# Three edits to the first stage of a fused sparse-attention and MoE kernel: which queue carries the weight words, where one copy stands, and which rounds convert weights

## The chip, the cores and the metric

The kernel runs on one core of a Trainium2 chip. Five engines with instruction streams of their own work side by side: TensorE (PE, matrix products; its weight loads are listed as PEld), VectorE (DVE), ScalarE (ACT), GpSimd (POOL) and SyncE (SP). Each executes its stream strictly in order. Loads and stores are carried by 16 DMA engines; SP, ACT and POOL issue them, and what each of the three issues stands in a queue of its own (q1 for SP, q10 for ACT, q0 for POOL). The metric is the device time of one execution in microseconds (us); lower is better.

## The reference, cut to what matters

```
scores = q @ k.T / sqrt(64)            # 4 batches, 8 heads, 768 positions, 64 wide
mask: own and neighbouring blocks of 32, first and last block, 3 sampled blocks per block;
      the first and the last block see everything
attn = softmax(scores where mask) ;  x = attn @ v          # x: 3072 tokens x 512
h = x @ w_in                                               # 512 -> 2048
g = h * sigmoid(1.702 * h)
out = g @ w_out                                            # 2048 -> 512
```

All products are made to full float32 accuracy by splitting operands into a high and a low part of a reduced format, so that one product is three matmuls.

## The kernel before, in words

Attention is cut into units of 64 query rows. A unit of the first and last block is dense and is worked in two items; every other unit is sparse and is one item. An item has scores (L342 dense, L332 sparse, on PE), a row maximum (`least`: L355 or L349 and its negation `nm`, on DVE), exponentials (`exps`, L366 or L363, on ACT), transposes through PE (L381) whose results ACT copies out of PSUM as tiles `pt` (L387), values (L419 dense, L410 sparse, on PE), a normalisation (L426 to L436, DVE), and a turn of the finished x (L443 on PE, then the high part on ACT, L450, and the low part on DVE, L451).

The first stage (`first`) works 13 items: three in `opening`, then one loop round for each of items 3 to 12; below, a round has its item's number. Item 3 is the second half of a dense unit, items 4 and 5 are sparse, 6 to 9 dense, 10 to 12 sparse. A round n makes the scores and the maximum of item n, transposes and copies item n-1, turns a finished unit, makes item n's exponentials and the values of item n-2 (in the last three rounds also of item n-1).

Between these stand the weights' operations. The generator `weights` turns w_in and w_out (64-bit words, so loaded as tiles `raw` of twice the size) into pairs of high and low parts. Each tile takes four steps: a shift on DVE (L524), a merge on DVE (L526) after which ACT's first pass (L486) of the next tile is put down, the low part of the tile before (L494), and a second merge on DVE (L535) after which ACT's cast (L501) is put down. ACT's share and the loads of later tiles wait in a list, `late`, that `flush` empties, at the latest at a round's end. w_out's merged tile is also stored to a scratch tensor `ws` (L503). Five tiles' conversions and a little are done in the first stage; the rest is spread over the first 16 steps of the second stage, which runs the MoE products (L574 to L576 up, L621 to L626 down) densely on PE with the remaining sparse items in between.

The words are loaded by ACT's queue in both stages (L476). All other loads of the first stage, those of the keys (`kres`, `kg`), the queries (`qt`), the dense values (`vown<-in_vd_dram`) and the middle rows (`vmid`), stand in SP's queue; the gathered rows of v come by POOL's. A load waits until its buffer is free and until the load eight before it, of SP's and ACT's together, has landed.

Of the kernel before, what the change touches and what calls it, by code (L numbers as in the profile page):

```python
# [54 lines left out]
class Kernel:  # L55
# [93 lines left out]
    def indices(self):  # L149
# [8 lines left out]
        def take(shape):  # L158
            n = 1
            for k in shape:  # L160
# [9 lines left out]
        nc.vector.tensor_copy(out=d[0:1], in_=self.sbr)  # L170
        vblk = take([NB])
        first, second = slice(1, NB - 2, 2), slice(2, NB - 1, 2)
        nc.gpsimd.iota(vblk[3 * BLK:P, first], pattern=[[2, NU]], base=-NB, channel_multiplier=0,
                       allow_small_or_imprecise_dtypes=True)
# [31 lines left out]
        for i in range(NR):  # L206
            for cols, rows in ((first, slice(BLK * i, BLK * (i + 1))), (second, slice(BLK * (i + 1), BLK * (i + 2)))):
                nc.vector.tensor_copy(out=vblk[rows, cols], in_=rr[rows, cols, i])
# [248 lines left out]
    def weights(self):  # L457

        nc = self.nc
        todo = []  # L460
        for f in range(NF + LAG):
            if f < NF:
                todo.append((f, 0))
            if f >= LAG:
                todo.append((f - LAG, 1))
        self.ready = set()
        tiles = {}

        scalar = self.late.append
        asked = [0]  # L470

        def fetch(k):
            def go(k, own):
                f, i = todo[k]
                raw = self.raw4 if own else self.words.tile([P, 2 * DM], I32, name="raw", bufs=3)
                nc.scalar.dma_start(out=raw, in_=self.w64[i][f])  # L476
                tiles[k] = {"raw": raw.rearrange("p (a b) -> p a b", b=2)}

            for n in range(asked[0], min(k + 1 + self.early, len(todo))):
                scalar(lambda n=n, own=self.early and n % 4 == 3: go(n, own))  # L480
                asked[0] += 1

        def first(k):
            def go():
                a = tiles[k]["a"] = self.words.tile([P, DM], I32, name="a", bufs=3)
                nc.scalar.activation(out=a.bitcast(F32), in_=tiles[k]["raw"][:, :, 1].bitcast(F32), func=AF.Abs, scale=REBASE)  # L486

            if k < len(todo):
                scalar(go)

        def last(k):
            f, i = todo[k]
            t, w = tiles[k]["t"], tiles[k]["a"].bitcast(F32)
            nc.vector.tensor_tensor(out=t[:, DM:2 * DM], in0=w, in1=t[:, 0:DM].bitcast(F32), op=ALU.subtract)  # L494
            self.ready.add((f, i))

        def high(k):
            def go():
                f, i = todo[k]
                t, w = tiles[k]["t"], tiles[k]["a"].bitcast(F32)  # L500
                nc.scalar.copy(out=t[:, 0:DM], in_=w)  # L501
                if i == 1:
                    nc.scalar.dma_start(out=self.ws[f], in_=w)  # L503
                tiles[k]["high"] = True

            scalar(go)

        fetch(0)
        yield
        fetch(1)  # L510
        first(0)
        yield
        for k, (f, i) in enumerate(todo):
            while i == 1 and f - WRING > self.downs - 1:
                yield
            fetch(k + 2)
            if i == 0 and f == NWIN:
                self.opening.close()
                late = self.pool("late", 1)
                self.win += [late.tile([P, 2 * DM], F32R, name=f"win{n}") for n in range(NWIN, NF)]  # L520
            if "a" not in tiles[k]:
                self.flush()
            raw, a = tiles[k]["raw"], tiles[k]["a"]
            nc.vector.tensor_scalar(out=a, in0=a, scalar1=3, scalar2=None, op0=ALU.logical_shift_left)  # L524
            yield
            nc.vector.scalar_tensor_tensor(out=a, in0=raw[:, :, 1], scalar=-0x80000000, in1=a, op0=ALU.bitwise_and,  # L526
                                           op1=ALU.bitwise_or)
            first(k + 1)
            yield
            if k > 0:  # L530
                if "high" not in tiles[k - 1]:
                    self.flush()
                last(k - 1)
            yield
            nc.vector.scalar_tensor_tensor(out=a, in0=raw[:, :, 0], scalar=29, in1=a, op0=ALU.logical_shift_right,  # L535
                                           op1=ALU.bitwise_or)
            tiles[k]["t"] = self.win[f] if i == 0 else self.wout[f % WRING]
            high(k)
            yield
        self.flush()  # L540
        last(len(todo) - 1)
# [381 lines left out]
    def first(self):  # L923

        items = [g for g in self.items if g["unit"]["n"] <= CU]

        def finish(todo):
            while todo:
                todo.pop(0)()

        def weights(k):
            for _ in range(k):
                next(self.conv)

        pending, turns = [], []

        def values(upto):
            while pending and pending[0]["n"] <= upto:
                g = pending.pop(0)
                finish(self.values(g))  # L940
                if g["end"]:
                    turns.append(g)

        def opening():
            a, b, c = items[:3]
            least, *exps = self.scores(a)
            next(self.index)
            more, *other = self.scores(b)
            finish([least])
            finish(exps)  # L950
            finish([more])
            finish(other)
            next(self.index, None)
            weights(1)
            self.flush()
            self.loads()
            least, *exps = self.scores(c)
            finish([least])
            next(self.index, None)
            for m in range(3):  # L960
                self.turned(a, m)()
            copy = self.turned(b, 0)
            finish(exps)
            copy()
            finish(self.values(a))
            for m in (1, 2):
                self.turned(b, m)()
            next(self.index, None)
            pending.extend((b, c))
            self.flush()  # L970
            self.loads()

        opening()
        for n, g in enumerate(items):
            if n < 3:
                continue
            sparse, before = self.sparse(g), items[n - 1]
            least, *exps = self.scores(g)
            finish([least])
            copies = self.transposes(before)  # L980
            copies.pop(0)()
            while turns:
                finish(self.turn(turns.pop(0)))
            if not self.sparse(before):
                copies.append(self.turned(before, 2))
            if not sparse:
                finish(exps)
            weights(1 if sparse else 2)
            values(n - 2)
            finish(copies)  # L990
            if sparse:
                finish(exps)
            if n >= len(items) - 3:
                values(n - 1)
            weights(0 if sparse else 2 if n == 3 else 1)
            pending.append(g)
            self.flush()
            self.loads()
        self.held = False
        finish(self.transposes(items[-1]))  # L1000
        while turns:
            finish(self.turn(turns.pop(0)))
        self.flush()
        self.loads()
# [105 lines left out]
```

## Time and profile before

| | |
|---|---|
| median of 3 runs | 727.14 us (726.73 to 727.65) |
| profiled execution, its own time | 729.48 us |
| its span, first to last instruction | 727.7 us |
| TensorE busy | 709.0 us (97% of the span) |
| VectorE busy | 450.3 us (62%) |
| ScalarE busy | 388.1 us (53%) |
| granted TensorE clock, mean | 0.998 |
| first stage: first MoE matmul starts at | 72.85 us |

The profiled execution's own time is 1.8 us longer than its span and 2.3 us over the median. A busy TensorE is not yet a TensorE at its peak, since matmuls overlap and their ends are modelled; the idle times and the chain of waits say more than the busy share.

### The profile page before, as it was taken

The page shows a single profiled execution, that of the slowest core. Times are in us where ns is not written, and L with a number is a line of the kernel's source. Part 1 is how long each engine was busy: PE and PEld are TensorE (multiplying, and loading weights), DVE is VectorE, ACT ScalarE, POOL GpSimd, SP SyncE. Part 2 cuts the span into 40 slices and gives each one's busy share as a digit, 9 for nine tenths or more (in the row PEclk, how much of TensorE's full clock was granted, in tenths as well). Part 3 has the DMA queues.
Part 4 walks back from the last instruction along what each step waited for, and adds up shares of the span by engine and source line. Part 5 has one row for each costly group of instructions (what it writes and reads, how often), then busy time and mean ns, then how long its engine had stood idle before and what let it go on. Part 6 is the DMA issues. An engine that isn't in the chain of part 4 may idle for free.

```text
span 727.7 us, 18730 instructions
## 1 busy us (share of the span) xinstructions
PE 709.0 (97%) x7554; PEld 560.9 (77%) x7554; DVE 450.3 (62%) x839; ACT 388.1 (53%) x760; POOL 62.5 (9%) x106
## 2 busy tenths in 40 slices
PE   7988999999999999999999999999999999999996
PEld 5656787887777877787778777877778788888885
DVE  5686989898545444454444444544677877676552
ACT  5776777676544544454445445544335554545442
POOL 3254101101100111111001111100000000000000
PEclk9999999999999999999999999999999999999999
DMA  8996877877576665567465545811111311011532
GB/s 349 411 400 228 261 264 247 276 260 259 155 224 198 184 210 176 178 215 224 121 201 170 191 146 178 238 47 43 33 52 35 87 30 45 30 43 30 145 116 72
DMA packets 58568, 123.16 MB, mean 169 GB/s; under 512 B 6961, under 2 KB 24626, under 8 KB 58482
## 3 DMA queue, kind: packets, MB, share of 16 engines
q1 hardware_dynamic: 44768, 76.91, 33.7%
q0 software_dynamic: 6336, 23.43, 9.6%
q10 hardware_dynamic: 7378, 21.63, 8.4%
q8 instruction: 59, 0.97, 0.5%
q14 instruction: 27, 0.22, 0.1%
HBM read 111.46 MB, written 10.49 MB: 168 GB/s over the span
## 4 chain that ended last, share of the span: by engine, by line
PE 83%; DVE 7%; ACT 5%; DMA 3%; issue 1%; ACTq 0%; SPq 0%; DVEq 0%
PE banks L621 11%; PE banks L625 11%; PE banks L626 11%; PE banks L837 10%; PE banks L574 7%; PE banks L575 7%; PE banks L576 7%; PE banks L381 6%; PE banks L410 6%; PE banks L332 5%; DMA raw<-in_moe_w_in_dram 1%; PE banks L443 1%; DVE mx L355 1%; PE banks L419 1%; PE banks L342 1%
## 5 line engine op out<-in xcount | busy, mean ns | idle before, releaser
L625 PE MATMUL banks<-wout,ghi 128*128 128x512 f32 x384 | 151.6, 395 | 0.0
L626 PE MATMUL banks<-wout,ghi 128*128 128x512 f32 x384 | 149.8, 390 | 0.1
L363 ACT ACTIVATE ex<-banks,nm 128x256 f32<-128x256 f32 x176 | 69.0, 478 | 76.1 <-DVE rg L426 53.3
L621 PE MATMUL banks<-wout,glo 128*128 128x512 f32 x384 | 107.6, 395 | 1.2 <-DVE glo L602 1.2
L563 DVE TENSOR_TENSOR wout<-wst,wout 128x512 fp32r<-128x512 f32 x80 | 55.2, 690 | 68.6 <-ACT wout L562 68.0
L582 ACT ACTIVATE g<-banks 128x512 f32<-128x512 f32 x64 | 38.3, 599 | 87.5 <-PE banks L576 87.5
L625 PEld LDWEIGHTS banks<-wout,ghi 128*128 128x128 f32 x384 | 72.1, 188 | 15.9 <-ACT ghi L594 0.4
L621 PEld LDWEIGHTS banks<-wout,glo 128*128 128x128 f32 x384 | 70.7, 188 | 17.4 <-DVE glo L602 2.8
L626 PEld LDWEIGHTS banks<-wout,ghi 128*128 128x128 f32 x384 | 72.2, 188 | 14.9 <-DVE wout L494 0.6
L574 PE MATMUL banks<-x,win 128*128 128x512 f32 x192 | 78.7, 410 | 0.1
L387 ACT COPY pt<-banks 128x512 f32<-128x512 f32 x112 | 61.0, 587 | 27.5 <-PE banks L381 27.1
L575 PE MATMUL banks<-x,win 128*128 128x512 f32 x192 | 75.2, 392 | 0.0
L576 PE MATMUL banks<-x,win 128*128 128x512 f32 x192 | 75.1, 391 | 0.0
L272 POOL DMA_INDIRECT vown<-in_v_dram,vidx x44 | 42.3, 962 | 371.7 <-PE banks L410 359.4
L589 DVE SCALAR_TENSOR_TENSOR g<-g,banks 128x512 f32<-128x512 f32 x51 | 35.0, 687 | 59.1 <-ACT g L582 58.9
L594 ACT CAST ghi<-g 128x512 fp32r<-128x512 f32 x80 | 50.0, 625 | 36.7 <-DVE g L589 30.6
L349 DVE TENSOR_REDUCE mx<-banks 128x4 f32<-128x1024 f32 x44 | 53.7, 1221 | 24.1 <-PE banks L332 24.0
L381 PEld LDWEIGHTS banks<-ident,ex 128*128 128x128 f32 x436 | 49.5, 140 | 15.3 <-ACT pt L387 4.9
L381 PE MATMUL banks<-ident,ex 128*128 128x128 f32 x436 | 58.0, 275 | 2.6 <-ACT pt L387 2.3
L410 PEld LDWEIGHTS banks<-vown,pt 128*32 128x32 f32 x1408 | 42.3, 109 | 19.7 <-issue 15.4
L562 ACT CAST wout<-wst 128x512 fp32r<-128x512 f32 x80 | 50.5, 631 | 9.8 <-DMA wst<-ws 7.9
L602 DVE TENSOR_TENSOR glo<-g,ghi 128x512 fp32r<-128x512 f32 x80 | 54.9, 686 | 0.7
(127 smaller groups left out, 1145.3 us busy)
## 6 DMA issues: line engine op xcount, KB each, us to landing
wst<-ws SPq DMA_DIRECT2D x80, 256.0 KB
kg<-in_kb_dram SPq DMA_DIRECT2D x126, 128.0 KB
raw<-in_moe_w_in_dram ACTq DMA_DIRECT2D x16, 512.0 KB
raw<-in_moe_w_out_dram ACTq DMA_DIRECT2D x16, 512.0 KB
kg<-in_kb_dram SPq DMA_DIRECT2D x18, 384.0 KB
vown<-in_vd_dram SPq DMA_DIRECT2D x8, 780.0 KB
qt<-in_q_dram SPq DMA_DIRECT2D x22, 256.0 KB
out_dram<-ot SPq DMA_DIRECT2D x40, 128.0 KB
```

The source lines that it names most:

```text
L363: nc.scalar.activation(out=ex[:, cols], in_=sps[h][:, cols], func=AF.Exp, bias=un["nm"][:, c:c + 1], scale=SCALE)
L381: self.nc.tensor.transpose(ps[:, slot], g["ex"][h][:, k * P:(k + 1) * P], self.ident)
L387: self.nc.scalar.copy(out=pt, in_=ps)
L410: nc.tensor.matmul(sums[BLK * c:BLK * (c + 1), 2 * i + h], g["pt"][h][:, 2 * i + k, BLK * c:BLK * (c + 1)], src[:, at:at + DV], start=(k = ...
L563: self.nc.vector.tensor_tensor(out=t[:, DM:2 * DM], in0=w, in1=t[:, 0:DM].bitcast(F32), op=ALU.subtract)
L574: nc.tensor.matmul(h, wih[:, k], hi[:, k], start=(k == 0), stop=False)
L575: nc.tensor.matmul(h, wih[:, k], lo[:, k], start=False, stop=False)
L576: nc.tensor.matmul(h, wil[:, k], hi[:, k], start=False, stop=(k == NCT - 1))
L621: nc.tensor.matmul(o[n], glo[:, tk[n]], woh, start=False, stop=last)
L625: nc.tensor.matmul(o[n], ghi[:, tk[n]], woh, start=(f == 0), stop=False)
L626: nc.tensor.matmul(o[n], ghi[:, tk[n]], wol, start=False, stop=False)
L837: self.nc.tensor.matmul(bank, a[:, k], b[:, k], start=start and k + n == 0, stop=k == 1 and n == 2, skip_group_check=True)
```

## The change

While the first stage runs (`self.early`), the loads of words and the stores of w_out's merged tile go into SP's queue in place of ACT's. In rounds whose predecessor is sparse, the second copy of its transposes is put right behind the first, ahead of the copies of the turned x. And the steps of the weights' generator are spread over the rounds 3 to 12 as 2,1,1,2,2,3,3,3,3,3 (24 with the opening's one), where they were 4,1,1,3,3,3,3,1,1,1 (22).

```diff
-                nc.scalar.dma_start(out=raw, in_=self.w64[i][f])
+                (nc.sync if self.early else nc.scalar).dma_start(out=raw, in_=self.w64[i][f])
...
-                    nc.scalar.dma_start(out=self.ws[f], in_=w)
+                    (nc.sync if self.early else nc.scalar).dma_start(out=self.ws[f], in_=w)
...
+            parts = []
             while turns:
-                finish(self.turn(turns.pop(0)))
+                parts += self.turn(turns.pop(0))
+            if self.sparse(before):
+                finish(copies)
+            finish(parts)
...
-            weights(1 if sparse else 2)
+            weights(2 if 8 <= n and not sparse else 1)
...
-            weights(0 if sparse else 2 if n == 3 else 1)
+            weights(2 if n >= len(items) - 3 else 0 if 3 < n < 6 else 1)
```

SP's queue, from the opening's loads on (`kg_101` are the keys of the dense units worked in rounds 6 and 7, `vmid_110` the middle rows of the first sparse items, `raw` the words; + is new):

```order
 L221 DMA qt_103<-in_qd_dram 128x256
 L235 DMA kg_101<-in_kT_dram 128x1536 x2
+L476 DMA raw<-in_moe_w_in_dram 128x1024 x2
 L270 DMA vmid_110<-in_vm_dram 128x1040
+L476 DMA raw<-in_moe_w_out_dram 128x1024
+L476 DMA raw_126<-in_moe_w_in_dram 128x1024
 L265 DMA vown_109<-in_vd_dram 128x1560
 L265 DMA vown_108<-in_vd_dram 128x1560
```

The first words now stand behind `kg_101` in the one queue, and the middle rows behind two loads of words.

ACT's stream in rounds 3 and 4, before:

```order
L366 ACTIVATE ex<-banks,nm 128x768 x2
L476 DMA raw<-in_moe_w_out_dram 128x1024
L486 ACTIVATE a<-raw 128x512
L476 DMA raw_126<-in_moe_w_in_dram 128x1024
L387 COPY pt_128<-banks 128x512
L387 COPY pt_129<-banks 128x512
L486 ACTIVATE a<-raw 128x512
L387 COPY pt_130<-banks 128x512
L450 CAST x_123<-banks 128x4x64
```

And the same place in the changed kernel, where the exponentials and the copies are those of the same items:

```order
L366 ACTIVATE ex<-banks,nm 128x768 x2
L387 COPY pt_128<-banks 128x512
L387 COPY pt_129<-banks 128x512
L486 ACTIVATE a<-raw 128x512
L387 COPY pt_130<-banks 128x512
L450 CAST x_123<-banks 128x4x64
L387 COPY pt_131<-banks 128x512
L387 COPY pt_132<-banks 128x512
L363 ACTIVATE ex<-banks,nm 128x256 x4
L486 ACTIVATE a<-raw 128x512
```

The first pass over the first words has moved behind round 3's copies, still ahead of round 4's first copy, `pt_130`; that over the second words moved behind round 4's exponentials.

DVE's stream from round 10's second merge to round 11's row maximum, before:

```order
L526 SCALAR_TENSOR_TENSOR a<-raw,a 128x512
L426 TENSOR_SCALAR rg<-banks 128x4
L427 RECIPROCAL rg<-rg 128x4
L436 TENSOR_TENSOR x<-banks,rg 128x256
L349 TENSOR_REDUCE mx<-banks 128x2x2
```

And in the changed kernel, where it works on an earlier tile of words (`raw_126`):

```order
L526 SCALAR_TENSOR_TENSOR a<-raw_126,a 128x512
L426 TENSOR_SCALAR rg<-banks 128x4
L427 RECIPROCAL rg<-rg 128x4
L436 TENSOR_TENSOR x<-banks,rg 128x256
L494 TENSOR_TENSOR wout_120<-a,wout_120 128x512
L535 SCALAR_TENSOR_TENSOR a<-raw_126,a 128x512
L349 TENSOR_REDUCE mx<-banks 128x2x2
```

The low part of a w_out tile and a merge now stand behind the normalisation and directly ahead of round 11's row maximum; before, they stood in round 9.

## Rows read from the trace of the kernel before

**Rows 1.** The page: TensorE's clock in 40 slices, the last chain by engine.

```profile
PEclk9999999999999999999999999999999999999999
...
PE 83%; DVE 7%; ACT 5%; DMA 3%; issue 1%; ACTq 0%; SPq 0%; DVEq 0%
```

**Rows 2.** The chain of waits in the first 95 us: start, length, what.

```profile
24.71 0.59 ACT pt L387
...
27.55 1.02 PE banks L332 x32
...
31.15 1.61 PE banks L342 x16
...
72.85 0.43 PE banks L574
```

**Rows 3.** DMA queues from 0 to 14 us: packets, MB, share of 16 engines.

```profile
q1 hardware_dynamic: 1417, 4.45, 82.3%
```

**Rows 4.** DMA queues from 10 to 14 us.

```profile
q1 hardware_dynamic: 394, 1.67, 102.0%
```

**Rows 5.** DMA queues from 14 to 22 us.

```profile
q1 hardware_dynamic: 435, 2.27, 68.6%
q10 hardware_dynamic: 284, 1.04, 32.2%
```

**Rows 6.** DMA queues from 22 to 30 us.

```profile
q1 hardware_dynamic: 452, 1.85, 57.0%
q0 software_dynamic: 213, 0.82, 25.5%
q10 hardware_dynamic: 163, 0.60, 18.9%
```

**Rows 7.** The page's DMA issues: what, queue, count, KB (of 1024) each.

```profile
raw<-in_moe_w_in_dram ACTq DMA_DIRECT2D x16, 512.0 KB
...
vown<-in_vd_dram SPq DMA_DIRECT2D x8, 780.0 KB
...
kg<-in_kT_dram SPq DMA_DIRECT2D x4, 768.0 KB
```

**Rows 8.** SP's own waits, 0 to 74 us: total, times, longest.

```profile
SPq L265 <- DMA vmid<-in_vm_dram: 3.4, 1, 3.4
```

**Rows 9.** SP in order of time, 14 to 36 us; a load that waited for words.

```profile
23.94 3.98 SPq L265 DMA_DIRECT2D vown<-in_vd_dram  x2
```

**Rows 10.** ACT in order of time, rounds 3 and 4: start, length.

```profile
22.29 0.66 ACT L486 ACTIVATE a<-raw 128x512 f32<-128x512 f32 x1
22.84 1.06 ACT L387 COPY pt<-banks 128x512 f32<-128x512 f32 x2
```

**Rows 11.** ACT in order of time, exponentials of rounds 6 and 7.

```profile
34.39 1.70 ACT L366 ACTIVATE ex<-banks,nm 128x768 f32<-128x768 f32 x2
...
39.29 1.83 ACT L366 ACTIVATE ex<-banks,nm 128x768 f32<-128x768 f32 x2
```

**Rows 12.** PE in order of time, round 8's scores.

```profile
42.31 1.52 PE L342 MATMUL banks<-kg,qt 64*64 64x384 f32 x16 [1.51 <-ACT pt L387]
```

**Rows 13.** DMA queues from 0 to 40 us.

```profile
q1 hardware_dynamic: 2968, 11.39, 71.3%
...
q0 software_dynamic: 288, 1.07, 6.6%
```

**Rows 14.** ACT in order of time, round 11's copies.

```profile
61.45 0.59 ACT L387 COPY pt<-banks 128x512 f32<-128x512 f32 x1 [2.39 <-PE banks L381]
...
62.38 0.59 ACT L387 COPY pt<-banks 128x512 f32<-128x512 f32 x1
```

**Rows 15.** DVE in order of time, round 10's end.

```profile
59.84 0.16 DVE L426 TENSOR_SCALAR rg<-banks 128x4 f32<-128x4 f32 x1 [2.67 <-PE banks L419]
```

**Rows 16.** The chain of waits at the second stage's last conversion.

```profile
173.88 0.50 PE banks L626
174.38 0.23 PE banks L625
```

## The prediction

> **What bounds the kernel now.** I read the page first. The chain that ended last lies on PE for 83%, with the clock at full in all 40 slices [rows 1], so the second stage is one dense row of matmuls and cannot be touched by this change other than by when it starts: its first matmul stands at 72.85 us [rows 2]. Every microsecond by which the first stage ends earlier or later is one on the result. Then the chain of waits over that stage: between 24.71, a copy of transposes on ACT at the head of round 4, and 31.15, round 6's scores, it runs without a gap over PE, and 3.6 us lie between the scores of round 5 (27.55) and those of round 6 [rows 2]. There is no slack in that stretch to absorb a late start. Third, the DMA queues, since two of the three edits move loads. From 0 to 14 us q1 (SP's) moved 4.45 MB [rows 3], from 10 to 14 it alone moved 1.67 MB, 0.417 MB per us, at 102% of the engines' time [rows 4]. From 14 to 22, q10 (ACT's, the words) took 1.04 of 3.32 MB although SP had loads waiting [rows 5], and from 22 to 30 the three queues share 3.27 MB [rows 6], 0.41 per us. The engines are full from 10 us on: a load is late by what stands ahead of it, and having a queue of one's own is worth a turn. Last, ACT's rows of rounds 3 and 4 and SP's waits.
>
> **Term A, the first words arrive later and ACT stands.** Before, the words of the first two tiles have a turn of their own: their 2 x 512 KB [rows 7], 1.05 MB, are just what q10 moved from 14 to 22 [rows 5], and a load of SP's that waited for the second of them could go at 23.94 [rows 9]. So a load is seen as landed about 1.9 us after its bytes have moved. ACT's first pass over them (22.29) did not wait [rows 10]. In the changed kernel they stand in q1 behind `kg_101`. Ahead of them are five loads' worth of the first keys, 4 x 768 KB, four dense value loads of 780 KB, two key loads of 768 KB [rows 7], which is 3.15 + 3.20 + 1.57 MB, and 0.52 MB of queries, 8.44 MB by the sizes in the issues and the program; with the first words themselves 8.96 MB. q1 has moved 4.45 at 14 us. Alone, at 0.417 per us, it has the rest, 4.51 MB, moved at 24.8. But the gathered rows of v begin to move at 22 to 23 us and take a quarter of the engines where three queues share (0.82 of 3.27 MB, and none before 22 [rows 5, 6]). I take 0.15 MB per us from 22.8 on: by then 8.12 MB are through, and 0.84 MB at 0.27 per us takes 3.1 us, so 25.9, and landed at 27.8. Bounds: landed at 26.7 with no share for the gathers, at 29.2 if all the 1.07 MB that q0 has moved by 40 us [rows 13] go ahead.
>
> The pass over these words now stands behind round 3's two copies, which end near 23.4 (22.84 plus 1.06 less the 0.45 that the pass ahead of them took), and ahead of round 4's first copy. ACT is in order, so it stands from 23.4 to 27.8; the pass takes 0.7, and the copy starts at 28.5 in place of 24.71 [rows 2, 10]. Queued behind it on ACT are the turned x, the other copies and round 4's exponentials; on DVE the shift of these words (L524) now stands ahead of round 4's row maximum and waits for the same pass; PE waits for the copy, because the next transposes use the bank that it empties. None of that had slack [rows 2]. **Plus 3.8 us; bounds 2.7 and 5.2.** The second pass, behind round 4's exponentials, comes about 4 us later and finds its words.
>
> **Term B, rounds 6 to 8.** The second copy behind the first puts the turned x and the exponentials of round 6 back by the spacing of a pair of copies, about 0.5. They ran from 34.39 to 36.09 and released round 7's scores. Round 7's exponentials, 39.29 to 41.12 [rows 11], shift by some 0.3 (the low part L494 and the merge that stood between on DVE have moved away). But round 8's scores did not start at 41.16 where these exponentials set them free; they started at 42.31 [rows 12]. The view names a copy, which the scores don't read; what they read is the first half of `kg_100`, whose last byte is at 11.48 MB of q1, and q1 had moved 11.39 by 40 us [rows 13]; with the 1.9 us above, that is 42.2. So the keys were last. In one queue these keys have two words loads less ahead of them, of the five that ACT had already moved, and term A gives them 3.8 us more: they are there. Also the middle rows, for which a load of SP's waited 3.4 us before [rows 8], stand behind two words loads instead of sharing with four. So round 8's scores start at 41.45 plus term A: **minus 0.9; bounds minus 1.2 (no shift in round 7) and 0 (something else holds them).**
>
> **Term C, the issue on ACT.** ACT issues no loads of words any more. Those issues ran beside exponentials already under way, so I take 0; the keys were early anyway, since round 6's scores follow the values without a gap [rows 2].
>
> **Term D, the last three rounds.** Round 11 had its copies at 61.45 and 62.38, with the turned x between [rows 14]. Right behind the first, the second starts 0.47 earlier, and the values, which wait for it, too; the same in round 12: 0.9 us at most. Against it, six more steps. Those on DVE at round 10's end start when the values release the normalisation at 59.84 [rows 15]: 0.8 for it, then two operations of 0.6 to 0.7, so round 11's maximum starts at 61.9 rather than 60.9, its exponentials end 0.5 later, and one more pass of 0.7 on ACT stands ahead of round 12's first copy. That takes back about 0.4. **Minus 0.5; bounds minus 0.9, all covered, and plus 1.3, one pass and one low part in the open.** The cover is the 2.67 us that DVE and the 2.39 us that ACT idle there [rows 14, 15].
>
> **Term E, the second stage.** It starts two generator steps ahead. Its last conversion is the only one that PE saw: a matmul took 0.50 at 173.88, where the next took 0.23 [rows 16]. **Minus 0.3; bound 0.**
>
> SP's queue has new waits: the fifth words (for round 6's merge on DVE) with a query tile and the values of round 11 behind it, and the first store of w_out (for round 9's) with round 12's queries behind it. Each is used 9 us or more after such a wait ends, and a load of that size takes 2 to 4 us once the engines are no longer full, so I cost them at nothing; uncovered, such a load is 2 to 4 us.
>
> **The sum.** 3.8 - 0.9 + 0 - 0.5 - 0.3 = +2.1 us. The profiled execution took 729.48, so 731.6 for its like; on the median of 727.14 it is 729.2.
>
> **Rivals.** *Words in time.* If the queue of issue made no difference to when loads land, ACT would not stand, the copy at 24.71 would come 0.5 earlier, and the sum would be -0.5 - 0.9 - 0.5 - 0.3 = -2.2: 724.9, faster. The row on q10 speaks against it: words issued at 12 us were through by 22 while SP's earlier loads still moved [rows 5]. It decides from the point where the first words land before 25.7, for there term A is worth the 1.7 of the others. The Trainium skill ("DMA: Bandwidth & Descriptors", Issuing engines are not separate DMA queues) says just this, that all issuers share the same 16 engines, interleave, and that several issuers save issue time alone. The same page (Queues, rings and completion order) has each engine take turns between queue rows, with order kept inside a row, and the q10 row agrees.
>
> *The two sides cancel.* Words at the early bound (2.7) and the other terms at theirs (-1.2, -0.9, -0.3) leave +0.3: 727.4. For it speaks that the keys' wait of round 8 is plainly in the trace [rows 12, 13]; against it that four terms have to lie at one end.
>
> *The clock falls as well.* ACT's stand leaves PE idle for about 4 us, from round 4's first transposes to its first copy, more than any wait of the stage before, of which the longest I found is 1.51 at full clock [rows 1, 12]. If the clock went to its lower level, the next 4 us of matmuls would take up to twice as long; take half of that, +2.8 with the slower restart: 732.0. The Trainium skill ("TensorE: Matmul & The Clock Gate", Why this matters for your kernels) warns of such a drop after idle gaps between bursts; no row of this case shows one.
>
> **How the numbers follow.** Chances: the forecast 0.42, with its own range of 727.9 to 731.0 (about half of each term's bounds); words in time 0.22; cancelling 0.25; the clock 0.11. A measurement of this kernel tells about 0.2%, 1.5 us, from no change. Slower: the forecast's part over 728.6, 0.36, and the clock, 0.11: 0.47. Faster: words in time and a little of the cancelling case: 0.24. The rest, 0.29, is the same. The range takes in all but the outer halves of the two extreme cases: 724.8 to 732.0.
>
> **What would show it.** In the changed kernel's rows: ACT's first pass (L486) waits for `raw` for 3 to 6 us, and lands near 27.8; the copy behind it starts near 28.5; round 5's scores are near 31.4; round 8's start with the exponentials' end and not with a load; round 11's two copies stand side by side; the first MoE matmul is near 75. If L486 doesn't wait, term A is wrong and the sign with it. If it waits and the first MoE matmul is nevertheless at 73 or before, the recovery in rounds 6 to 12 is larger than terms B and D.

## The result, and the profile after

The changed kernel is slower: 733.97 us median (733.07 to 735.05, 4 runs) against 726.93 us (726.71 to 727.65, 4 runs), a ratio of 1.0088, 95% interval 1.0064 to 1.0113 (the two medians alone divide to 1.0097, inside it). By the medians that is 7.0 us more where 2.1 were forecast. The profiled execution took 733.71 us, 4.2 more than that of before (729.48), which stood 2.6 above the median of 726.93; a second pair of traces below takes up that difference.

The page of the changed kernel, TensorE's clock in 40 slices and the last chain by engine, to be held against [rows 1]:

```profile
PEclk9899999999999999999999999999999999999999
...
PE 87%; DVE 4%; DMA 4%; ACT 3%; issue 1%; ACTq 0%
```

One slice, the second (18 to 37 us), has lost clock, and DMA has gained a per cent on the chain. ACT in order of time over rounds 3 and 4 (start, length, in brackets the idle time ahead and what ended it), for [rows 10]:

```profile
22.37 1.06 ACT L387 COPY pt<-banks 128x512 f32<-128x512 f32 x2
29.23 0.66 ACT L486 ACTIVATE a<-raw 128x512 f32<-128x512 f32 x1 [5.80 <-DMA raw<-in_moe_w_in_dram]
29.80 0.57 ACT L387 COPY pt<-banks 128x512 f32<-128x512 f32 x1
```

ACT stands 5.80 us for the first words, and round 4's first copy, at 24.71 before [rows 2], starts at 29.80. The waits from 20 to 40 us (engine, line, what for: total, times, longest) show who stands behind it:

```profile
PE banks L381 <- ACT pt L387: 5.8, 2, 5.5
DVE a L524 <- ACT a L486: 6.4, 1, 6.4
ACT a L486 <- DMA raw<-in_moe_w_in_dram: 5.8, 1, 5.8
```

PE by stretches (stretch, its length, PE's busy time and matmuls, granted clock, DMA share, GB/s):

```profile
core 0: us, PE busy (x), PEclk, DMA share, GB/s
22.00:26.00 4.00, 2.91 (x64) 1.00 1.02 410
26.00:30.00 4.00, 0.00 (x0) 0.68 1.02 411
30.00:34.00 4.00, 3.58 (x50) 0.50 1.03 419
34.00:38.00 4.00, 4.00 (x100) 0.97 0.76 253
```

PE has no matmul from 26 to 30; the granted clock falls in that stretch, and from 30 to 34 PE works at 0.50, the lower of its two levels, 1.2 GHz. The chain of waits (start, length, what), for [rows 2, 12]:

```profile
14.05 15.15 DMA raw<-in_moe_w_in_dram
...
30.42 1.12 PE banks L381 x4
31.53 2.80 PE banks L419 x48
34.33 1.02 PE banks L332 x32
...
37.93 1.54 PE banks L342 x16
...
46.69 1.04 PE banks L410 x64
47.73 0.46 PE banks L342
...
64.86 0.60 DVE wout L494
65.46 0.81 DVE a L535
...
66.30 0.02 ACT win L501
...
66.82 0.83 ACT pt L387 x2
...
77.30 0.43 PE banks L574
```

The chain now begins with the load of words. Round 5's scores (L332) are at 34.33, 6.8 us later than the 27.55 of [rows 2], and round 6's at 37.93 as many. Round 8's scores (47.73) follow the values directly; they are 5.4 later than in [rows 12], so 1.4 has been won back on the way. Between rounds 10 and 11 stand a low part, a merge and a cast of weights (64.86 to 66.8). The first MoE matmul is at 77.30 for 72.85.

Last, the DMA queues of the changed kernel (packets, MB, share of 16 engines), first from 0 to 26 us, then from 22 to 30 as in [rows 6]:

```profile
q1 hardware_dynamic: 2406, 8.95, 86.1%
q0 software_dynamic: 110, 0.46, 4.4%
...
q1 hardware_dynamic: 542, 2.20, 67.6%
q0 software_dynamic: 286, 1.06, 33.3%
```

By 26.0 us q1 had moved 8.95 MB, as many bytes as end with the first words (8.96 by the prediction's count); the words were landed 3.2 us later.

### The profile page after: what moved, and what is told of

It reads as the page before. It is cut to its first block, busy times and chain, and to the rows that moved or that the text cites. A ratio compares the mean times of both kernels' runs of the same rounds, so it can differ in the third digit from the quotient of the medians.

```text
span 731.9 us, 18736 instructions
## 1 busy us (share of the span) xinstructions
PE 712.4 (97%) x7554; PEld 562.8 (77%) x7554; DVE 450.1 (61%) x839; ACT 388.3 (53%) x760; POOL 63.1 (9%) x106
## 4 chain that ended last, share of the span: by engine, by line
PE 87%; DVE 4%; DMA 4%; ACT 3%; issue 1%; ACTq 0%
PE banks L621 12%; PE banks L625 11%; PE banks L626 11%; PE banks L837 10%; PE banks L574 8%; PE banks L575 7%; PE banks L576 7%; PE banks L381 6%; PE banks L410 6%; PE banks L332 6%; DMA raw<-in_moe_w_in_dram 2%; PE banks L419 1%; PE banks L443 1%; DMA kres<-in_kT_dram 1%; DVE gs L760 1%; PE banks L342 1%
## 5 line engine op out<-in xcount | busy, mean ns | idle before, releaser
L626 PE MATMUL banks<-wout,ghi 128*128 128x512 f32 x384 | 149.7, 390 | 0.0
L563 DVE TENSOR_TENSOR wout<-wst,wout 128x512 fp32r<-128x512 f32 x80 | 55.2, 690 | 69.2 <-ACT wout L562 66.8
L626 PEld LDWEIGHTS banks<-wout,ghi 128*128 128x128 f32 x384 | 72.1, 188 | 14.8 <-DVE wout L494 0.3
```

Source lines behind the costliest of these rows:

```text
L563: self.nc.vector.tensor_tensor(out=t[:, DM:2 * DM], in0=w, in1=t[:, 0:DM].bitcast(F32), op=ALU.subtract)
L626: nc.tensor.matmul(o[n], ghi[:, tk[n]], wol, start=False, stop=False)
```

## The experiments

Theory 1: the first words queue behind `kg_101`, ACT stands, and PE's clock falls because PE idles; the other edits give back 2 to 3 us. Theory 2: the loss lies in the last rounds' steps or in the copies. Theory 3: one queue in place of two costs the time, wherever the words stand in it. The later runs are compared by ratio, since the kernel before took 729.9 to 730.4 us in them.

**The words back on ACT's queue, the rest as changed.**

```diff
-(nc.sync if self.early else nc.scalar).dma_start(out=raw, in_=self.w64[i][f])
+nc.scalar.dma_start(out=raw, in_=self.w64[i][f])
...
-(nc.sync if self.early else nc.scalar).dma_start(out=self.ws[f], in_=w)
+nc.scalar.dma_start(out=self.ws[f], in_=w)
```

> The changed kernel with the words and the stores of w_out issued by ACT again; the second copy and the new spread of steps stay. Theory 1 (the first words queue behind keys in SP's queue, so ACT stands 5.8 us in round 4 and PE's clock falls after it; about 7 us lost, 2 to 3 won back elsewhere): no wait of L486 for raw over 0.5 us, no slice of the first stage with a granted clock under 0.95, round 5's scores near 27.5, and a median of 725 to 727. Theory 2 (the loss is in the last rounds, where six more steps of weights stand, or in the copies side by side): 732 to 734, with round 5's scores near 27.5 and the loss after round 8.

Measured: 729.0 us against 729.87, ratio 0.9985 (0.9976 to 0.9994); the first pass at 23.0 without a wait, clock 1.00 in all stretches from 14 to 46 us. Theory 2 is out: with copies and steps as changed the kernel is a little faster than before. The 725 to 727 expected, with 2 to 3 us won back, was missed: the kernel before took 3 us more here than in the first runs, and the ratio gives 1.1 us back.

**The queue alone.** The two lines above, changed the other way, in the kernel before.

> The kernel before with only the words and the stores of w_out moved to SP's queue; copies and steps as before. Theory 1: the first pass L486 stands from about 22.3 for the words until near 29, and here the copies of round 3's transposes may stand behind it too, so the loss is that of the whole change or more: 733 to 738. Theory 2 (last rounds or copies): 726 to 728.

Measured: 737.16 us, ratio 1.0094 (1.0076 to 1.0112). Here the pass stands ahead of round 3's copies too, and ACT waits longer than in the changed kernel, as its row in order of time says:

```profile
29.07 0.66 ACT L486 ACTIVATE a<-raw 128x512 f32<-128x512 f32 x1 [7.06 <-DMA raw<-in_moe_w_in_dram]
```

The granted clock is 0.50 from 26 to 34 us. This one edit makes the whole loss.

**The words in SP's queue, but ahead of `kg_101`.**

```diff
         self.knext, self.vnext = RING + 1, RING + 2
+        next(self.conv)
+        self.flush()
         self.loads()
...
             next(self.index, None)
-            weights(1)
             self.flush()
```

> The changed kernel, all loads of words still in SP's queue, but the first two issued ahead of the first keys outside the ring (kg_101) in place of behind them. Theory 1 (the place in the one queue decides): the words land near 22.5 by the bytes ahead of them, L486 waits less than 1 us, and the time is 725 to 728; kg_101 lands some 2.5 us later and may hold round 6's or 7's scores by up to 1 us. Theory 3 (that all of it goes through one queue in place of two costs the time, wherever the words stand): 732 to 734.

Measured: 729.0 us, ratio 0.9983 (0.9974 to 0.9992). ACT in order of time has the first pass without a wait:

```profile
23.13 0.71 ACT L486 ACTIVATE a<-raw 128x512 f32<-128x512 f32 x1
```

And the chain has the scores of rounds 6 and 8 and the first MoE matmul:

```profile
30.86 1.55 PE banks L342 x16
...
40.68 1.97 PE banks L342 x16
...
71.98 0.43 PE banks L574
```

The same queue for words and stores, another place for the first words, and the loss is gone; `kg_101`, now behind the words, holds nothing (PE runs from round 5's scores into round 6's without a gap). Theory 3 is out. The Trainium skill ("DMA: Bandwidth & Descriptors", Issuing engines are not separate DMA queues) says that issuing from several engines saves issue time alone. Read with the place kept, these runs agree (0.9983 with one queue, 0.9985 with two); read as "it does not matter who issues", the changed kernel contradicts it, for a change of queue is also a change of place.

**The words between the halves of `kg_101`.** As above, with `load_k(..., range(1))` ahead of the words and `load_k(..., range(1, 2))` behind them.

> The first two words loads issued between the two halves of kg_101 in SP's queue: ahead of the first words stands 0.77 MB less than in the changed kernel and 0.77 MB more than in the kernel with the words first. Theory 1 by bytes: q1 of the changed kernel had moved 7.78 MB at 22 us and 0.275 MB per us after it, the first words are through at 8.19 MB, so they land near 25.4, ACT stands about 2 us from 23.4, and round 4's transposes behind its first copy start near 26.6 (25.05 with the words first, 30.42 in the changed kernel). If the clock holds over the shorter idle time of PE, the median is about 1.5 us over that of the words first: a ratio of 0.999 to 1.001 to before. If the clock falls here too, about 1 us more. If the place did not matter by bytes, it would stand at either end, 0.998 or 1.009.

Measured: 731.67 us against 729.99, ratio 1.0008 (0.9991 to 1.0026). SP's queue from 0 to 23 us:

```profile
q1 hardware_dynamic: 2280, 8.23, 90.1%
```

ACT in order of time:

```profile
25.62 0.66 ACT L486 ACTIVATE a<-raw 128x512 f32<-128x512 f32 x1 [2.42 <-DMA raw<-in_moe_w_in_dram]
```

PE by stretches:

```profile
24.00:26.00 2.00, 0.86 (x8) 1.00 1.03 418
26.00:28.00 2.00, 1.19 (x24) 1.00 1.02 401
```

And the chain behind the wait:

```profile
26.81 0.66 PE banks L381 x4
```

Landing (25.62 for 25.4), transposes (26.81 for 26.6) and loss over the words first (0.0025 of 730, 1.8 us for 1.5) come out near what was expected, though the ratio is good to 1.3 us only and the landing is right by luck: the bytes were through before 23.0 where 23.5 was expected, and the landing came 2.7 later where 1.9 was taken. PE idles about 1.9 us here, and the clock holds at 1.00.

**The words where the change put them, the first pass later.** No steps in rounds 3 and 4; rounds 3 to 12 take 0,0,1,3,3,3,3,3,3,4.

```diff
-            weights(2 if 8 <= n and not sparse else 1)
+            weights(0 if n < 5 else 1 if n == 5 else 2 if n < 10 else 1)
...
-            weights(2 if n >= len(items) - 3 else 0 if 3 < n < 6 else 1)
+            weights(3 if n == 12 else 2 if n >= len(items) - 3 else 0 if n < 6 else 1)
```

> The changed kernel with the words where the change put them, behind kg_101, but with no steps of weights in rounds 3 and 4; the steps left out stand in rounds 5 to 9 and one in 12, so that as many are done when the second stage starts. Theory 1 (the words are late only because the first pass stands at round 4's head): ACT no longer stands in round 4, the clock holds, round 6's scores come near 30.9, and the time is 1 us below before to 1 us above, ratio 0.9985 to 1.0015. If a later place only moves the stand (the next words then wait behind keys and values further back), the scores of a later round are late by 3 us or more and the ratio is 1.004 to 1.009.

Measured: 729.74 us, ratio 0.9991 (0.9978 to 1.0005); the first pass at 31.47 without a wait, round 6's scores at 30.97, clock 1.00. The words land as late as in the changed kernel (28.98 by the trace's semaphore records), but ahead of their first use. Late words cost nothing that these runs can tell where the pass that needs them stands later still.

**PE kept busy while ACT stands.** The products are not used.

```diff
             copies = self.transposes(before)
+            if n == 4:
+                for _ in range(22):
+                    self.nc.tensor.matmul(self.bank[2][:, 3 * P:4 * P], self.ident, self.ident, start=True, stop=True)
             copies.pop(0)()
```

> The changed kernel with 22 matmuls of 128 columns added between round 4's first transposes and its first copy, into a part of a bank that nothing reads at that time; their results are not used. They keep PE busy for part of the time in which ACT stands for the words. Theory 1 with the clock: ACT's wait for raw stays at 5.8 us, the stretches 26 to 38 us show a higher granted clock than 0.68, 0.50 and 0.97, the four transposes behind the wait take under 0.8 us in place of 1.12 and round 4's 48 value matmuls near 1.6 in place of 2.8; the median is 1.7 us lower, near 732.3. If the clock is worth nothing, the time stays at 734; if the filled time is too short to hold the clock, the granted clock falls all the same and the time stays too.

Measured: 734.84 us against 729.87, ratio 1.0064 (1.0049 to 1.0080). ACT waits for the words as long as before (5.91 us). PE by stretches:

```profile
26.00:30.00 4.00, 3.91 (x36) 1.00 1.02 408
30.00:34.00 4.00, 3.63 (x88) 1.00 1.04 421
34.00:38.00 4.00, 4.00 (x73) 1.00 1.01 378
```

And the chain:

```profile
30.37 0.66 PE banks L381 x4
31.02 1.55 PE banks L419 x48
...
36.17 1.55 PE banks L342 x16
```

The same wait without the fall of the clock: transposes 0.66 for 1.12, values 1.55 for 2.80, round 6's scores at 36.17 for 37.93. The clock's part is 1.8 us against the first trace of the change and 2.4 against the second (38.58, below); the ratios (1.0088 less 1.0064) say 1.8, though their intervals overlap.

**Both kernels traced again, on one chip.**

> The kernel before, unchanged, for a second trace taken on the same chip as the one below of the changed kernel. It tells whether the two traces shown so far, whose times differ by 4.2 us where the medians differ by 7.0, came from executions that can be set side by side. If the trace of before is typical, round 9's 1.2 us in which DVE and ACT start late behind PE's transposes (50.08) is there again, and the first MoE matmul stands near 72.9.

> The changed kernel, unchanged, traced on the same chip as the one above. Theory 1: the stand of 5.8 us, the clock of 0.5 after it and the scores of round 6 near 37.9 come again; if round 9's 1.2 us is a property of the chip and not of the kernel, it is here too, and the first MoE matmul comes near 78.5 in place of 77.3, so that the two traces differ by about 6 us, as the medians do. If it is the changed kernel that avoids it, the first MoE matmul stays near 77.3.

Measured: 730.25 us for before (one execution), and 736.39 us median for the change, ratio 1.0088 (1.0067 to 1.0109); the two traced executions, 730.25 and 735.62, are 5.4 apart, nearer to what the medians say. The trace of before came again, with the first MoE matmul at 72.89. The chain of the changed kernel's second trace has round 4's first copy, the scores of rounds 6 and 9, round 10's transposes and the first MoE matmul:

```profile
29.44 0.58 ACT pt L387
...
38.58 1.52 PE banks L342 x16
...
53.81 1.45 PE banks L342 x16
...
60.85 1.09 PE banks L381 x8
...
79.30 0.43 PE banks L574
```

The last is 2.0 later than in the first trace: round 9's scores to round 10's transposes took 7.04 us, as in before (7.03: 54.33 less 47.30), and 5.95 in the first trace (59.12 less 53.17), and the clock stayed low longer. The stretches of this second trace:

```profile
26.00:30.00 4.00, 0.00 (x0) 0.91 1.02 406
30.00:34.00 4.00, 3.94 (x60) 0.50 1.04 421
34.00:38.00 4.00, 4.00 (x74) 0.73 0.84 291
```

So the first trace of the change was 1.1 us quicker in round 9. Only two other traces are as quick there, those of the two spreads at this section's end; why DVE and ACT start some 1.1 us late there in all the rest stays open.

**The second copy alone, and the steps alone**, each in the kernel before; the lines are those of the change.

> The kernel before with the second copy of sparse transposes right behind the first, and nothing else. By my sum it saves up to 0.9 us in rounds 11 and 12 and costs up to 0.3 in rounds 6 to 8, whose second copies put exponentials back: 0.5 us faster, ratio 0.9985 to 1.0000. Theory 2 (copies or steps carry the loss): slower by over 2 us.

> The kernel before with the new spread of weights' steps alone: six more in the last rounds, fewer in rounds 6 to 8, words on ACT's queue. By my sum: round 8's scores come up to 0.9 us earlier, since fewer loads of words stand beside its keys; the last rounds cost 0.4 to 1.2 more, since a low part, a shift and a pass on the way from round 10 to 11 are no longer covered: a ratio of 0.9990 to 1.0010. Theory 2: slower by over 2 us.

Measured: 729.72 us, ratio 0.9991 (0.9974 to 1.0007), and 729.22 us, ratio 0.9982 (0.9966 to 0.9998), both against 730.4. The copy alone can't be told from nothing. The steps alone are as good as both together (0.9985 with the words on ACT): round 8's scores come at 40.95 in place of 42.31, the first MoE matmul at 72.16.

**Two other spreads with the words first.** In the first the last line reads `2 if n >= len(items) - 2 else 0 if n == 4 else 1` (one step from round 10 to round 5), in the second `2 if n >= len(items) - 3 else 0 if n == 4 else 1` (one step more, 25).

> The kernel with the words first, with one step of weights less at round 10's end and one more at round 5's. In the kernel with the words first the chain from round 10 to 11 goes over a low part, an OR and a cast of weights (59.54 to 61.6), as it does in the changed kernel. If those steps are worth 0.7 us there, the first MoE matmul comes near 71.3 in place of 71.98 and the ratio is 0.997 to 0.998 of before; if the second stage's last words bound the end instead, it stays at 0.998 to 0.9985.

> The kernel with the words first, with one step of weights more (at round 5's end), 25 in place of 24 before the second stage. It tests term E: if the second stage gains by steps done ahead, PE's wait for the last low part near 173.7 (1.2 us with the words first) shrinks and the second stage is shorter by 0.2 to 0.9 us, ratio 0.997 to 0.998. If that wait is set by when the words land there, nothing changes: 0.998 to 0.9985.

Measured: 728.61 us, ratio 0.9979 (0.9962 to 0.9997), and 729.72 us, ratio 0.9992 (0.9977 to 1.0007). The first has its first MoE matmul at 71.62, 0.36 earlier than with the words first, where 0.7 was expected; its ratio can't be told from 0.9983. Nor are the 0.36 the step's: round 9 is one of the quick ones, so that round 10's last four transposes start 1.0 earlier (53.51 for 54.52), and of that 0.65 is lost again behind them. The second's wait in the second stage stays, as the waits from 140 to 200 us say of it:

```profile
PE banks L626 <- DVE wout L494: 0.9, 1, 0.9
```

With the words first and 24 steps it is 0.8; a step more ahead does not shorten it, and the time is not better.

## Why the prediction failed

The sign, the place and the chain of waits were right; the size was not. Two steps of the sum failed: the fall of the clock stood at nothing in it, as a rival with 0.11, and term A had the words landed too early. Behind them, term D's gain was smaller than forecast.

Against before, the second trace of the change is 7.4 us later at round 6's scores (38.58 for 31.15), 6.5 at round 9's (53.81 for 47.30) and 6.45 at the first MoE matmul (79.30 for 72.85); the sum had 3.8, 2.9 and 2.4 there. Of the 7.4, 4.7 are the stand (29.44 for 24.71), and 2.7 come between that copy and round 6's scores, while the clock is low. In the first trace it is 6.8, of which 5.1 and 1.7. By ratios on 730 us, good to about 1 us each, the stand is 5.9 (1.0064 less 0.9983; 4.9 to 5.3 by those traces), the clock 1.8, all else -1.2 (0.9983 less 1), together 6.4 or 0.88%.

**Term A, +3.8 forecast.** It measured 5.1 and 4.7 in the two traces, under its upper bound of 5.2. The bytes were right: 25.9 us was worked out for the end of the first words, and q1 had as many moved at 26.0. The time from there to landed was not: 1.9 us, read from one load that waited for words and from the edge of a stretch [rows 5, 9], was 3.2 here and 2.7 with the words between the halves (8.23 MB at 23.0, landed 25.6, for 8.19 needed).

The trace's semaphore records, which no view prints, show why. A load adds 16 steps to its semaphore, as many as there are DMA engines, and ACT goes on with the last. Of the first words' steps the first came at 26.00, the twelfth at 26.55, the fifteenth at 27.79 and the last at 29.21. So three quarters of the load were there soon after the bytes said so, and one straggler held ACT 1.4 us longer than all the others. Before had such stragglers too: its first words had half their steps by 19.04 and the last at 20.67, 1.6 later, but the first half of `kg_101` had half by 25.05 and the last at 28.43, 3.4 later. The lag at the time in question could be had from the kernel before, and it was not 1.9. A queue's total also counts what was moved of later loads, so it can't show a straggler. What makes one share late, and on which engine, is not shown. Nor does the landing at the upper bound speak for the reason given for that bound: by 26 us the gathers had moved 0.46 MB, close to the 0.15 per us that was assumed, and not all of their 1.07, though it was 1.05 by 29.2.

**The clock, a rival at 0.11.** It fell, as that rival said: PE stood 5.5 us for the copy and then ran at 0.50. The forecast left the fall out of its sum and priced it in the rival at 2.8, from no row; it cost 1.7 and 2.7 in the two traces. Its chance was too low for two reasons: the stand was undersized, and "no row of this case shows one" was taken as evidence against, although PE in before had no wait that long in these rounds (1.51 at most [rows 12]). The Trainium skill ("TensorE: Matmul & The Clock Gate", Why this matters for your kernels) warns of the drop after idle gaps; the idle times of 1.9 us at 1.00 and 5.5 us down to 0.50 agree with it.

**Term B, -0.9 forecast.** Right, by the steps: in the kernel with the steps alone round 8's scores start 1.36 earlier, over the bound of 1.2, and round 9's still 0.9 earlier (46.39 for 47.30 in the chains). With the copy alone, which leaves the words loads ahead of `kg_100` as they were, round 8 starts at 42.04, close to 42.31. That the keys were last there was read from bytes; the semaphore records bear it out. The last step of the first half of `kg_100` came at 42.22 in before, where the scores start at 42.31, at 41.95 (42.04) with the copy alone and at 40.85 (40.95) with the steps alone, just as the values end.

**Term C, 0.** Nothing seen against it: ACT's next work starts 0.80 us after the second exponentials' start in both kernels (22.29 after 21.49, 22.37 after 21.57).

**Term D, -0.5 forecast.** Most of the gain was not there. From round 10's transposes to the first MoE matmul it is 18.52 us before, 18.18 and 18.45 in the two traces of the change, and 18.79 with the words first (71.98 less 53.19), so -0.3 to +0.3, inside the bounds. By single traces the copy alone has 18.42 there and the steps alone 18.75: the copies gave 0.1 and not 0.9, and the steps took back 0.2. The wait was the one foreseen, a low part, a merge and a cast.

**Term E, -0.3 forecast.** It can't be told from the result. From the first MoE matmul to the end of the span it is 654.9 and 655.6 in the two traces of before, 654.6 and 654.5 in those of the change, but 654.6 to 657.8 with the same 24 steps in seven other kernels: other things move it by more than the term. The wait that the term was read from did shrink in the change (L626, 0.50 before, is 0.41 and 0.33), but with the words first it is longer. The premise that each microsecond of the first stage is one on the result held only roughly: 0.9 us at the first MoE matmul with the words first was 0.1 in its span (727.6 for 727.7), though 1.2 by the ratio.

## What to carry to other kernels

Moving a load to another issuing queue moves it behind everything that queue still holds: add up those bytes, add the lag of the last of its 16 shares as the profile at hand shows it for loads of that time, and ask which in-order engine will stand at the load's first use, and what stands behind it there. The cure may be the place in the queue or the place of the use; both were worth about 1%. Where a new wait leaves PE idle longer than any wait of the profile at hand, the full clock of that profile says nothing about what PE will do after it: price the fall into the forecast itself.

## What was not expected of the hardware

From q1's total reaching a load's end to its landing it took 2.7 and 3.2 us here, not the 1.9 taken from before, because one of the load's 16 shares came 1.4 to 1.7 us after all the others (29.21 after 27.79, 25.60 after 23.90). The clock after the same wait differed between executions: 0.97 from 34 to 38 us in one trace of the change, 0.73 in the other, and the four transposes that ran first after the wait took 1.12 and 1.11 us in place of 0.66.
